# Storing g in five parts as it is made, and turning one chunk earlier

## The chip, the core and the metric

The kernel runs on one NeuronCore of a Trainium2 chip. The metric is the device time of one execution in microseconds. An execution of the profiled kind also leaves a trace: every instruction of every engine with its start and duration, every DMA packet, and the clock that TensorE was granted.

## What is computed

A retention block followed by a feed-forward block with squared ReLU. Cut to what matters:

```python
# q, k, v: (8, 8, 576, 64) float32 = batch, heads, sequence, head size
scores = q @ k.transpose(0, 1, 3, 2) / 8
Dmat = where(i >= j, gamma[h] ** (i - j), 0)          # causal decay, one gamma per head
x = ((scores * Dmat) @ v) -> (4608, 512)              # tokens x (heads * head size)
h = maximum(x @ w_in, 0)                              # w_in  (512, 2048)
out = (h * h) @ w_out                                 # w_out (2048, 512)
```

The two weight matrices arrive as 64-bit floats, so the kernel first makes 32-bit ones of them. The squared hidden layer is called g in the kernel.

## The kernel before, in words

**Retention.** Each of the 8 sequences is cut into four chunks of 128 tokens and one of 64, 40 chunks in all. A chunk's q and k are multiplied by powers of gamma (`scale_q`, `scale_v` on GpSimd; line 377 and 491), turned so that the head size lies across the partitions, multiplied with each other (`scores`), masked by VectorE (L484 or L543) and multiplied with v; a running state `u` carries what earlier chunks add. The first chunks are turned by TensorE (`turn_in`, L431) into PSUM and copied out by `turn_out` (L442: one half by ScalarE, one by VectorE); later ones are turned by VectorE (`flip`, L399) with small copies on ScalarE (L414). The result x goes, turned, to `xT` (L586).

**Weights.** The 64-bit weights come in pieces of 512 KB. A piece is converted in six steps (`round_parts`): two integer operations on VectorE (L212, L216), two operations on ScalarE (`beside`, L220 and L221), and three more on VectorE (L224, L227, L230). `convert(n)` emits the next n steps of the pieces of w_in in order. Pieces of w_out are converted later, summed, and kept in DRAM (`w2_dram`, stored at L283).

**First layer.** Tokens go in nine blocks of 512. Block 0 is multiplied directly (`first_in`, L714), piece by piece as w_in is converted. Blocks 1 to 8 use seven products in place of eight (`PRODUCTS`, `ffn_in`, L750): for each of four pairs of feature tiles `mp` there are seven steps `j`, each of eight matmuls of 128x128 by 256 columns. The steps' results are joined and squared into five parts of g: A11 (step 3: ScalarE L766, then squared by GpSimd L767), A22 (step 4: VectorE L769 and L757), S3 (step 5: L773, L757), A12 (step 6: L776, L757), and S1. Two sums follow, S1 = S3 + A22 (L690) and S3 = A11 - S3 (L691). The parts lie in `g_room`, which has room for two pairs, and go to `g_dram`.

**Second layer.** When all blocks are through, g is fetched again (`fetch_g`, L1016) and multiplied with w_out by the same seven products, once around and once within (`inner`, L1088). This part, from about 575 us on, touches neither edit.

**What sets the order.** The schedule is written out by hand: the order in which Python emits instructions is the order on each engine, and semaphores are added where one engine reads what another wrote. Chunks 0 to 3 and the first pieces of w_in are a plain list of calls (lines 889 to 947). From then on a loop over chunks takes a number of `step()`s of the first layer between the parts of a chunk's retention. Side work waits in `queue`; `some()` emits one entry of it in steps 6, 0, 1, 2 and 3. All loads and stores after the first three are issued by SyncE in the order of emission, so a store whose data are not ready holds up the loads behind it. In the trace SyncE has at most eight transfers under way: each issue waits for the landing of the eighth before it.

The loads for a chunk (`loads`) are emitted about three chunks before they are used.

## Time and profile before

| | us |
|---|---|
| time, median of three executions | 969.81 (969.76 to 970.41) |
| span of the profiled execution | 967.7 |
| TensorE busy | 949.6 |
| VectorE busy | 786.7 |
| ScalarE busy | 337.0 |
| GpSimd busy | 134.9 |
| bytes moved by DMA | 181.37 MB |
| g stores by `g_sums` | 32 of 1280 KB, 5.7 from issue to landing (median) |

Busy time is the time in which an engine had an instruction of the program under way. PE stands for TensorE's matmuls and PEld for its weight loads, DVE for VectorE, ACT for ScalarE, POOL for GpSimd, SP for SyncE; a q behind it (SPq) is its instruction queue. In the list of waits a line gives the engine and line that waited, what ended the wait, the total, the number of times and the longest. In a timeline a row gives start and duration in us, the engine, the line, the operation with output and input, the count, and in brackets the idle time before it with its releaser; "issue" means that the profile shows nothing the engine waited for. In a view by windows a row gives the stretch, its length, TensorE's busy time with the number of instructions, the granted clock as a share of the full one, the share of the DMA engines' time and the rate in GB/s.

### The profile page before, as it was taken

What the parts mean: (1) busy time and instruction counts of PE and PEld (TensorE: products, weight loads), DVE (VectorE), ACT (ScalarE), POOL (GpSimd) and SP (SyncE); (2) the same over time, 40 slices, a digit from 0 to 9 for tenths busy, and PEclk for the clock granted to TensorE, in tenths of its full rate; (3) what the DMA queues carried; (4) which work ended last, traced back from release to release, by engine and by line L of the source; (5) the groups of instructions that cost most, each with busy time, mean ns of one, the idle gap of its engine ahead of it and who ended that gap; (6) DMA issues with size and microseconds to landing.
All of it is one profiled execution on the core that took longest, in us unless ns stands there. A gap on an engine that the chain in (4) does not pass through costs nothing. (4 is left out here: it accounts for less than half of the span.)

```text
span 967.7 us, 23162 instructions
## 1 busy us (share of the span) xinstructions
PE 949.6 (98%) x9750; PEld 851.4 (88%) x9750; DVE 786.7 (81%) x1446; ACT 337.0 (35%) x807; POOL 134.9 (14%) x123
## 2 busy tenths in 40 slices
PE   8899999999999999989999999999999999999998
PEld 6654688888888888878888899999999999999998
DVE  5689799888799797977976597887888787887876
ACT  3354375856765766747721000000000000000000
POOL 3311323214223213222110000000000000000000
PEclk9999999999999999999999999999999999999999
DMA  9975567677757867755168966445354454525241
GB/s 230 239 215 138 151 180 197 192 238 197 199 153 223 242 162 190 230 168 169 61 247 333 358 244 266 149 159 185 122 196 160 159 198 166 199 100 174 88 175 44
DMA packets 170728, 181.37 MB, mean 187 GB/s; under 512 B 116864, under 2 KB 131200, under 8 KB 163968
## 3 DMA queue, kind: packets, MB, share of 16 engines
q1 hardware_dynamic: 168528, 179.37, 59.4%
q8 instruction: 76, 1.25, 0.5%
q10 hardware_dynamic: 2096, 0.52, 0.3%
q14 instruction: 28, 0.23, 0.1%
HBM read 109.36 MB, written 70.52 MB: 186 GB/s over the span
## 5 line engine op out<-in xcount | busy, mean ns | idle before, releaser
L750 PE MATMUL h_b<-room,w 128*128 128x256 f32 x768 | 184.7, 384 | 2.1 <-DVE room L769 1.8
L414 ACT COPY qk<-flip 32x256 f32<-32x256 f32 x416 | 167.4, 402 | 6.1
L750 PEld LDWEIGHTS h_b<-room,w 128*128 128x128 f32 x768 | 145.1, 191 | 24.5 <-DVE room L769 3.2
L1088 PE MATMUL o_b<-w,room 128*128 128x128 f32 x1168 | 144.4, 275 | 0.2 <-DVE room L1040 0.2
L1088 PEld LDWEIGHTS o_b<-w,room 128*128 128x128 f32 x1168 | 137.2, 192 | 0.4 <-DVE room L1040 0.4
L750 PE MATMUL h_a<-room,w 128*128 128x256 f32 x512 | 122.6, 382 | 2.7 <-issue 2.7
L1088 PE MATMUL o_c<-w,room 128*128 128x128 f32 x1008 | 123.0, 275 | 0.0
L750 PE MATMUL h_c<-room,w 128*128 128x256 f32 x512 | 121.7, 380 | 0.0
L1088 PEld LDWEIGHTS o_c<-w,room 128*128 128x128 f32 x1008 | 117.7, 192 | 0.0
L750 PEld LDWEIGHTS h_a<-room,w 128*128 128x128 f32 x512 | 96.6, 190 | 16.0 <-issue 2.6
L1102 ACT COPY r<-o_a 128x128 f32<-128x128 f32 x53 | 14.1, 265 | 271.7 <-PE o_a L1088 236.0
L750 PEld LDWEIGHTS h_c<-room,w 128*128 128x128 f32 x512 | 96.7, 190 | 13.3
L1088 PE MATMUL o_a<-w,a 128*128 128x128 f32 x688 | 85.6, 275 | 0.0
L767 POOL TENSOR_TENSOR room<-room 128x512 f32<-128x512 f32 x32 | 35.9, 1121 | 339.1 <-ACT room L766 339.1
L1088 PEld LDWEIGHTS o_a<-w,a 128*128 128x128 f32 x688 | 81.2, 192 | 0.1
L757 DVE SCALAR_TENSOR_TENSOR room<-room 128x512 f32<-128x512 f32 x96 | 70.7, 736 | 3.3
L714 PE MATMUL h_ps<-room,w 128*128 128x512 f32 (+2 forms) x160 | 60.7, 528 | 3.3 <-DVE w L230 3.0
L377 POOL TENSOR_TENSOR q_ld<-q_ld,dv 128x512 f32<-128x512 f32 (+1 forms) x39 | 46.2, 1185 | 85.2 <-DMA q_ld<-in_q_dram 77.5
L491 POOL TENSOR_TENSOR v_ld<-v_ld,dv 128x512 f32<-128x512 f32 (+1 forms) x40 | 53.5, 1338 | 6.7 <-DMA v_ld<-in_v_dram 6.7
L714 PEld LDWEIGHTS h_ps<-room,w 128*128 128x128 f32 x160 | 27.9, 199 | 27.5 <-issue 20.6
L609 PEld LDWEIGHTS x_ps<-qk,v_ld 64*64 64x64 f32 x1024 | 38.8, 134 | 13.0 <-issue 11.6
L769 DVE TENSOR_TENSOR room<-h_b,room 128x512 f32<-128x512 f32 x32 | 21.9, 685 | 33.5 <-PE h_b L750 33.5
(115 smaller groups left out, 1380.0 us busy)
## 6 DMA issues: line engine op xcount, KB each, us to landing
g_dram<-room SPq DMA_DIRECT2D x32, 1280.0 KB, 5.7
a<-g_dram SPq DMA_DIRECT2D x30, 1024.0 KB, 5.8
room<-g_dram SPq DMA_DIRECT2D x15, 1024.0 KB, 6.1
w<-w_dram SPq DMA_DIRECT2D x7, 1792.0 KB, 9.9
out_dram<-room SPq DMA_DIRECT2D x17, 512.0 KB, 3.3
q_ld<-in_q_dram SPq DMA_DIRECT2D x64, 128.0 KB, 5.3
w<-in_moe_w_in_dram SPq DMA_DIRECT2D x16, 512.0 KB, 6.3
w<-in_moe_w_out_dram SPq DMA_DIRECT2D x16, 512.0 KB, 4.2
```

The source lines that it names most:

```text
L377: engine.tensor_tensor(t, t, dv[:cs, :, NCH + ci:NCH + ci + 1].to_broadcast([cs, H, D]), op=ALU.mult)
L414: nc.scalar.copy(*moves.pop(0)[2:])
L491: nc.gpsimd.tensor_tensor(vs[:cs], vs[:cs], dv[:cs, :, ci:ci + 1].to_broadcast([cs, H, D]), op=ALU.mult)
L609: return [lambda hp=hp, e=e, b=b: nc.tensor.matmul(x_at(hp, e, b, h), lhsT=s["vs"][rows(h), head(hp, e), :], rhs=s["ret"][rows(h), e, hp, ...
L714: nc.tensor.matmul(p, lhsT=w[:, c, :], rhs=xT[0][:, c, :].rearrange("p (h t) -> p h t", h=2)[:, lo:hi, at[0]:at[1]], start=(c == 0), stop= ...
L750: nc.tensor.matmul(p[:, mm, :], lhsT=w[:, c, :], rhs=xs[n][right][:, c, :], start=(j in OPENS and mm == 0 and c == 0), stop=(j in CLOSES a ...
L757: nc.vector.scalar_tensor_tensor(t, t, 0.0, t, op0=ALU.max, op1=ALU.mult)
L767: nc.gpsimd.tensor_tensor(g["A11"], g["A11"], g["A11"], op=ALU.mult)
L769: nc.vector.tensor_tensor(g["A22"], p, p15, op=ALU.add)
L1088: nc.tensor.matmul(p, lhsT=s["lefts"][left][:, m, :], rhs=w_out[j][:, m, WO_SLOT[right], :], start=(i in OPENS and m == 0), stop=(i in CLO ...
L1102: nc.scalar.copy(r[:, 0, 0:128], p)
```

## The change

Two edits.

The first divides the store of g. Before, the last entry of `g_sums` stored all five parts of a pair at once, 1.28 MB. Now each part of 256 KB is stored in a step after it is made: A11 in step 5, A22 in step 6, A12 together with the sum S1, S1 together with the sum S3, and S3 last. The parts leave earlier and in smaller pieces, and the buffer's parts come free one by one.

The second moves chunk 3's turn in the list of calls. Before, four conversion steps of the third piece of w_in (`beside`, L224, L227, L230) stood ahead of it. Now the turn comes first, `beside` goes between turn and scores, and the three VectorE steps come after the scores. It is meant to let TensorE have the scores of chunk 3 without waiting for a conversion.

```diff
+    def g_store(n, mp, name):
+        nc.sync.dma_start(g_dram[n, G_KEPT.index(name), :, 2 * mp:2 * mp + 2, :], g_of(mp)[name])
+
     def g_sums(n, mp):
         g = g_of(mp)
         return [
-            lambda: nc.vector.tensor_tensor(g["S1"], g["S3"], g["A22"], op=ALU.add),
-            lambda: nc.vector.tensor_tensor(g["S3"], g["A11"], g["S3"], op=ALU.subtract),
-            lambda: nc.sync.dma_start(g_dram[n, :, :, 2 * mp:2 * mp + 2, :].rearrange("s p m t -> p s (m t)"),
-                                      g_room[mp % 2].rearrange("p s m t -> p s (m t)")),
+            lambda: [nc.vector.tensor_tensor(g["S1"], g["S3"], g["A22"], op=ALU.add), g_store(n, mp, "A12")],
+            lambda: [nc.vector.tensor_tensor(g["S3"], g["A11"], g["S3"], op=ALU.subtract), g_store(n, mp, "S1")],
+            lambda: g_store(n, mp, "S3"),
         ]
...
             queue.extend(g_sums(n, mp))
+
+        if j in (5, 6):
+            g_store(n, mp, "A11" if j == 5 else "A22")
...
     load(6)
-    convert(4)
     turn(3)
+    convert(1)
     scores_full(3)
     scale_q(4, nc.gpsimd)
+    convert(3)
     carry_full(3)
```

## The prediction

> **What bounds the kernel now.** I read the busy times first, then the list of TensorE's waits, then the timeline around the longest of them.

> The busy row of the page:
> ```profile
> PE 949.6 (98%) x9750; PEld 851.4 (88%) x9750; DVE 786.7 (81%) x1446; ACT 337.0 (35%) x807; POOL 134.9 (14%) x123
> ```
> TensorE works 949.6 of 967.7 us and no product is taken away. So the change can win only idle TensorE time, about 18 us, and time in which TensorE runs at a reduced clock, which counts as busy. TensorE's waits, total, times, longest:
> ```profile
> PE sc_ps L539 <- DVE qk L442: 3.6, 2, 3.4
> PE h_ps L714 <- DVE w L230: 3.0, 4, 1.2
> PE h_a L750 <- issue: 2.7, 1, 2.7
> PE h_b L750 <- DVE room L769: 1.8, 2, 1.3
> ```
> No line says that TensorE waited for a g store; the only reader of that kind is ScalarE, once, 1.3 us. Two single waits, 3.4 and 2.7 us, stand out.

> The first, in the timeline of TensorE (start, duration):
> ```profile
> 26.41 0.41 PE L431 MATMUL t_ps<-w,q_ld 64*128 64x64 f32 x8
> 30.18 1.16 PE L539 MATMUL sc_ps<-qk 64*128 64x128 f32 x16 [3.35 <-DVE qk L442]
> 31.27 1.13 PE L558 MATMUL x_ps<-qk,u_sb 64*64 64x128 f32 x16
> 32.33 3.14 PE L714 MATMUL h_ps<-room,w 128*128 128x128 f32 x16
> ```
> and of VectorE:
> ```profile
> 24.39 0.41 DVE L216 TENSOR_SCALAR w<-w 128x512 uint32<-128x512 uint32 x1
> 27.21 0.69 DVE L224 SCALAR_TENSOR_TENSOR w<-w,w 128x512 f32<-128x512 uint32 x1 [2.41 <-ACT w L220]
> 28.74 0.69 DVE L230 SCALAR_TENSOR_TENSOR w<-w,w 128x512 uint32<-128x512 uint32 x1
> 29.35 0.68 DVE L442 COPY qk<-t_ps 128x512 f32<-128x512 f32 x1
> ```
> Chunk 3 is transposed by 26.82, but VectorE copies it out only at 29.35: the copy stands behind three conversion steps, the first of which waits 2.41 us for ScalarE. After the gap the products are slow too: L558 takes 1.13 us here and 0.67 at 22.10; sixteen records of L714 take 3.14 here and 2.05 at 37.18. The windows show why (length, busy with its count, granted clock, DMA share, GB/s):
> ```profile
> 32.00:33.00 1.00, 1.00 (x11) 0.50 1.13 330
> 33.00:34.00 1.00, 1.00 (x7) 0.50 1.22 264
> ```
> and, after the second gap:
> ```profile
> 422.00:423.00 1.00, 1.00 (x4) 0.50 1.01 371
> ```
> The clock is halved in just two stretches before the end, each about 3.4 us long, one after each of the two gaps.

> The second gap has no releaser. TensorE's timeline, SyncE's, and the data queue between 410.94 and 416.6 us (packets, MB, share):
> ```profile
> 419.17 2.46 PE L750 MATMUL h_a<-room,w 128*128 128x256 f32 x8 [2.69 <-issue]
> ```
> ```profile
> 407.23 0.37 SPq L692 DMA_DIRECT2D g_dram<-room  x1
> 410.08 0.37 SPq L283 DMA_DIRECT2D w_dram<-w  x1
> ```
> ```profile
> q1 hardware_dynamic: 1128, 1.77, 101.9%
> ```
> Queue q8 carries instructions: 76 packets of 16 KB, and TensorE's 19,572 records make 76.5 blocks of 256. In the undisturbed last 350 us the k-th packet starts when TensorE is at record 256(k+0.64). Packet 37 should have started at 410.94; it started at 416.64, after 1.77 MB of data, took 1.03 us, and TensorE went on 1.5 us later. Until then it had run dry: it stopped at record 256(37+1.79), so packet k must be usable, 1.5 us after it ends, by 256(k+1.79). So this gap is a late instruction fetch, behind a g store of 1.28 MB (issued 407.23) and a store of converted weights of 1.34 MB (410.08).

> [...] A gap of 1.16 us at 19.85 to 21.01 us brought no drop. [...] here fetches waited until what was issued before them had gone (packet 18: a 1.79 MB store issued 0.25 us before its trigger, 7.17 us late; with nothing ahead, 0.8 to 1.3 us). [...]

> **Part 2: chunk 3's turn ahead of four conversion steps.** The order on VectorE becomes L216, copy L442, two mask products L543, then L224, L227, L230; ScalarE's copy likewise comes ahead of L220 and L221. Nothing is added. TensorE ends its transposes at 26.82; both copies start at once (at 7.92 and 7.95 they did so for chunk 0), VectorE's 0.69 us ends at 27.58, and the scores start 0.15 later, as now: 27.72 for 30.18, **2.46 us**. The gap left is 0.9 us, less than the 1.16 us that cost no clock, so L558 and L714 run at full speed: 1.13 - 0.67 and 3.14 - 2.05, **1.55 us**. Together 4.0.

> Who pays? The piece moved back (the third) ends at 32.2 to 33.0 us: masks from 28.88 to 30.17, then three steps of 0.6 to 1.5 us. Its reader, the third direct product, then stands at 39.80 - 4.0 = 35.8. The next piece would end some 5 us earlier than at present, against 4 for TensorE. Loads do not bind: the fifth and sixth chunks' q land at 36.39 and 40.12, and are turned at 43.7 and 53.5 even so.

> **Part 1: five stores.** Bytes and 2 KB rows are the same. Added: 128 issues at 0.37 us, 47 us of SyncE, which spends 151 us on issues between 110 and 575 us: nobody waits for it as such. A 256 KB store of g lands in 2.4 us (first quarters of block 0), the 1.28 MB one in 5.7. The buffers are rewritten two feature pairs later, over ten products of 1.73 us on, so the new waits of L690, L773 and L776 on landings, with the rest of VectorE's work queued behind them, are met long before; L769's such wait costs nothing visible now.

> SyncE's order does change. Three stores (A11, A22, A12) now stand ahead of a chunk's loads and wait for GpSimd and VectorE; behind them are q, k and v loads. At 410.5 the loads would move back to 416.7, when A12 is ready: 6 us. Who waits? GpSimd's scaling of q, which after 130 us begins 7 to 27 us after its landing, mostly over 10. At 117.65 the A11 store holds loads until 119.9, as GpSimd is itself waiting for q; k, landing at 125.8 now, is used at 130.26. So I charge nothing.

> The gain is at the late fetch. A22 and A12 leave by about 404 us, S1 and S3 by 404.5 and 407.2, so when the 1.34 MB store comes at 410.08 the queues are empty of g. That store remains whole ahead of the fetch: 1.34 MB at the 0.38 MB/us of its neighbouring slices is 3.5 us from 411.1, so the fetch begins near 414.7, is usable at 414.7 + 1.0 + 1.5 = 417.2, and TensorE, dry at 416.5, stands 0.7 us instead of 2.69: **2.0 us**. Such a short gap should not drop the clock: 2.46 - 1.99 and 3.05 - 1.89 for the two product groups after it, **1.7 us**. Bounds: nothing (the stall stays) and 2.7 + 1.7 = 4.4. Fetches with thin margins before that point (packets 17 and 31, 1.8 and 1.3 us) had g stores ahead of them, so they gain slack.

> Sum: 969.8 - 4.0 - 3.7 = **962.1 us**.

> **Rivals.** *Fetch still starved (0.20):* the weight store alone is enough to keep the gap and the clock drop; 969.8 - 4.0 = 965.8. For it: packet 18 was 7.17 us late with no g ahead. Against: the 0.4 MB of g ahead of packet 37 are gone. *Late loads (0.08):* moved back by 6 us, they reach VectorE's transposes late, as one k load does now (2.4 us at 116.5, without stopping TensorE); two or three such waits that do stop TensorE eat 1.5 to 4 us: 967.5 to 970. Against: the slack of 7 us or more. *Slower (0.06):* stores spread over the step lie ahead of more fetches; if the old stall stays and two more blocks starve at 4.4 us each, 965.8 + 8.8 = 974.6. Against: each store adds at most 0.7 us, and all fetches but three have over 2.7 us in hand.

> **How the numbers follow.** First forecast 0.66, around 962.1 (960.5 with the stall wholly gone plus some of VectorE's waits; 963.8 with half of it). It and the starved rival make 0.86, hence 960.5 to 966.3. Faster by over 0.2% means below 967.9: 0.66 + 0.20 and a third of the late loads, 0.89; same 0.05; slower 0.06.

> **What would show it.** The scores of chunk 3 start near 27.7 with a wait under 1 us, and the clock shows no drop near 31 to 35. The product that follows the gap at 419 comes 0 to 1 us after the one before, with no clock drop. Wrong would be: VectorE waiting for q or k loads, GpSimd's L767 late, or "issue" gaps on TensorE elsewhere.

## The result, and the profile after

| | before | after |
|---|---|---|
| time, median | 969.78 us (969.62 to 970.41, 4 runs) | 962.51 us (962.35 to 962.81, 4 runs) |
| ratio to before | | 0.9924 (0.9907 to 0.9941) |
| span of the profiled execution | 967.7 us | 960.6 us |

The change takes 7.3 us off; 7.7 were forecast, 962.1 us. The total came out closer than its parts: the term for the second gap was 1.1 us too large, and the profile of after is ahead by 0.7 us at its start, which no part of the change explains.

The busy row of the page of after, then TensorE's longest waits (total, times, longest):

```profile
PE 945.7 (98%) x9750; PEld 848.6 (88%) x9750; DVE 787.7 (82%) x1446; ACT 337.3 (35%) x807; POOL 135.4 (14%) x123
```
```profile
PE h_ps L716 <- DVE w L230: 2.2, 3, 1.6
PE h_a L752 <- issue: 1.8, 1, 1.8
PE h_b L752 <- DVE room L771: 1.8, 2, 1.3
PE sc_ps L539 <- DVE qk L442: 1.2, 2, 0.9
```

As many products as before, in 3.9 us less busy time: 3.2 us of that are the two stretches at half clock that are gone (the table below). Of the two waits that stood out, the one for chunk 3's scores has shrunk from 3.4 to 0.9 us; the one without a releaser is still there, at 1.8 us for 2.7.

Chunk 3 in TensorE's timeline, and in VectorE's (start, duration; idle time before in brackets):

```profile
25.69 0.41 PE L431 MATMUL t_ps<-w,q_ld 64*128 64x64 f32 x8
27.01 1.16 PE L539 MATMUL sc_ps<-qk 64*128 64x128 f32 x16 [0.91 <-DVE qk L442]
28.10 0.67 PE L558 MATMUL x_ps<-qk,u_sb 64*64 64x128 f32 x16
28.70 2.05 PE L716 MATMUL h_ps<-room,w 128*128 128x128 f32 x16
```
```profile
26.17 0.69 DVE L442 COPY qk<-t_ps 128x512 f32<-128x512 f32 x1 [1.53 <-PE t_ps L431]
...
29.38 0.68 DVE L224 SCALAR_TENSOR_TENSOR w<-w,w 128x512 f32<-128x512 uint32 x1
```

VectorE now waits for the transposes (1.53 us) instead of the reverse, copies at 26.17, and takes up the conversion, L224, after the masks. L558 and L716 take 0.67 and 2.05 us where they took 1.13 and 3.14. By windows (these rows have the busy times of all five engines; the clock is the third column from the right), the places of both old drops are at full clock:

```profile
33.00:34.00 1.00, 1.00 (x11) 1.00 (x10) 0.66 (x3) 1.00 (x3) 0.00 (x0) 1.00 1.35 229
415.00:416.00 1.00, 1.00 (x7) 0.87 (x6) 0.52 (x1) 0.31 (x1) 0.00 (x0) 1.00 0.77 174
```

The second gap in TensorE's timeline, SyncE's timeline ahead of it, and what the data queue moved between 406.39 us, when TensorE comes to record 256(37 + 0.64), at which the prediction's fit has fetch 37 due, and 411.36, when it starts:

```profile
413.77 1.46 PE L752 MATMUL h_a<-room,w 128*128 128x256 f32 x6 [1.84 <-issue]
```
```profile
403.18 1.17 SPq L687 DMA_DIRECT2D g_dram<-room  x2
405.54 0.37 SPq L283 DMA_DIRECT2D w_dram<-w  x1
406.44 6.07 SPq L687 DMA_DIRECT2D g_dram<-room  x3
```
```profile
q1 hardware_dynamic: 706, 1.93, 101.7%
```

The fetch still comes late, behind 1.93 MB in place of 1.77. It is 4.96 us late, not 5.69: the 1.77 MB included 624 packets of 256 bytes, pieces of loads, and went at 0.31 MB/us; the 1.93 had none and went at 0.39.

Where the time went, by comparing when TensorE reaches the same instruction in both traces:

| stretch | after is ahead by a further |
|---|---|
| up to 17 us, before either edit acts | 0.72 us |
| wait for chunk 3's scores | 2.45 us |
| first clock drop | 1.55 us |
| 60 to 95 us, TensorE waiting for conversions | -0.2 us |
| gap of fetch 37 | 0.85 us |
| second clock drop | 1.69 us |

The first row is no gain. The product of L714 (L716 in the changed kernel) that begins at 17.24 us before begins at 16.52 after; in six more profiles, of kernels that are the same up to there, it begins anywhere between 16.39 and 16.84 us. Between 60 and 95 us the lead rises and falls (5.54, 3.65, 4.50 us). A second profile of the changed kernel, `after_again` below, gains 0.1 us over the same stretch, so the -0.2 is no cost of the change either.

### The profile page after: what moved, and what is told of

Read it like the earlier page. It is cut to its first block, busy times and chain, and to the rows that moved or that the text cites. A ratio compares the mean times of both kernels' runs of the same rounds, so it can differ in the third digit from the quotient of the medians.

```text
span 960.6 us, 23424 instructions
## 1 busy us (share of the span) xinstructions
PE 945.7 (98%) x9750; PEld 848.6 (88%) x9750; DVE 787.7 (82%) x1446; ACT 337.3 (35%) x807; POOL 135.4 (14%) x123
## 5 line engine op out<-in xcount | busy, mean ns | idle before, releaser
L752 PE MATMUL h_b<-room,w 128*128 128x256 f32 x768 | 183.6, 382 | 2.1 <-DVE room L771 1.8
L752 PEld LDWEIGHTS h_b<-room,w 128*128 128x128 f32 x768 | 144.1, 190 | 23.9 <-DVE room L771 3.2
L752 PE MATMUL h_a<-room,w 128*128 128x256 f32 x512 | 122.0, 381 | 1.8 <-issue 1.8
L752 PE MATMUL h_c<-room,w 128*128 128x256 f32 x512 | 121.7, 380 | 0.0
L752 PEld LDWEIGHTS h_a<-room,w 128*128 128x128 f32 x512 | 96.4, 190 | 15.1 <-issue 1.7
L752 PEld LDWEIGHTS h_c<-room,w 128*128 128x128 f32 x512 | 96.7, 190 | 13.3
L769 POOL TENSOR_TENSOR room<-room 128x512 f32<-128x512 f32 x32 | 35.9, 1121 | 335.9 <-ACT room L768 299.4
L716 PE MATMUL h_ps<-room,w 128*128 128x512 f32 (+2 forms) x160 | 59.6, 518 | 3.5 <-DVE w L230 2.2
L716 PEld LDWEIGHTS h_ps<-room,w 128*128 128x128 f32 x160 | 26.8, 190 | 27.4 <-issue 20.7
```

Source lines behind the costliest of these rows:

```text
L716: nc.tensor.matmul(p, lhsT=w[:, c, :], rhs=xT[0][:, c, :].rearrange("p (h t) -> p h t", h=2)[:, lo:hi, at[0]:at[1]], start=(c == 0), stop= ...
L752: nc.tensor.matmul(p[:, mm, :], lhsT=w[:, c, :], rhs=xs[n][right][:, c, :], start=(j in OPENS and mm == 0 and c == 0), stop=(j in CLOSES a ...
L769: nc.gpsimd.tensor_tensor(g["A11"], g["A11"], g["A11"], op=ALU.mult)
```

## The experiments

Each kernel is set against runs of the kernel before on the same chip (medians 969.2 to 969.9 us).

**The two edits apart.** The first kernel has only the new place of the turn, the second only the five stores:

```diff
+    turn(3)
+    convert(1)
     scores_full(3)
     scale_q(4, nc.gpsimd)
+    convert(3)
```

> Chunk 3's turn moved, g still stored at once. Theory (the two edits act apart, the turn by 2.46 us of waiting and 1.55 us of halved clock): 969.8 - 4.0 = 965.8 us; the scores of chunk 3 wait about 0.9 us, the clock drop near 31 us is gone, and the gap of 2.7 us in the first layer (instruction fetch) with its clock drop is still there. Rival (VectorE is the bound between 48 and 110 us and gives the 4 us back there): 968.5 to 969.8. Rival (the gap in the first layer is a matter of chance and not of the stores): gap under 2 us without a clock drop, about 963.

> Five stores of g, chunk 3's turn where it was. Theory: the gap in the first layer shrinks from 2.7 to about 1.8 us and brings no clock drop, 0.9 + 1.7 = 2.6 us: 967.2 us; scores of chunk 3 still wait 3.3 us and the clock drops after it. Rival (the stores win by freeing buffers earlier or by easing the load on the queues all along): more than 2.6 us, with shorter waits in other places. Rival (the stores win nothing by themselves): 969.8.

The turn alone: 965.15 us (964.07 to 966.9), ratio 0.9957 (0.9944 to 0.997). The stores alone: 967.1 us (966.44 to 967.91), ratio 0.9973 (0.9963 to 0.9984). A line of the waits of the first kernel and a window of it, then the waits of the second:

```profile
PE h_a L750 <- issue: 2.7, 1, 2.7
```
```profile
417.00:418.00 1.00, 1.00 (x4) 0.81 (x3) 0.00 (x0) 0.75 (x2) 0.00 (x0) 0.50 1.04 381
```
```profile
PE sc_ps L539 <- DVE qk L442: 4.4, 2, 4.1
PE h_a L752 <- issue: 1.9, 1, 1.9
```

The parts separate: with the turn alone the gap of fetch 37 and its clock drop stay; with the stores alone the wait for the scores stays and the gap is 1.9. The gains, 4.2 and 2.3 us, sum to 6.5 of 7.3, which is within what these intervals tell. So the turn brought about 4 us, as forecast. The stores brought 2.3 us by time (1.6 to 3.6) and 2.5 by the table above, not 3.7.

**Is the gap a matter of where an instruction block ends?** Sixteen idle products of 32 columns, 64 instruction records of TensorE, move every later block boundary 64 records earlier. (A block is what one packet of q8 carries; over the last 350 us the packets start 255.7 records apart in the kernel before and 255.6 in the changed one.) A first pair put them into the warm-up in place of a product:

```diff
+    def small(count):
+        t = ps_f.tile([128, 512], F32, tag="f", name="idle_ps")
+        for _ in range(count):
+            nc.tensor.matmul(t[0:64, 0:32], lhsT=idle[:, 0:64], rhs=idle[:, 0:32], start=True, stop=True)
...
-    warm(5)
+    warm(4)
+    small(17)
```

> The kernel before with 64 more records on TensorE at its start, g stored at once and chunk 3 turned late as before. Theory (the gap of 2.7 us is a late instruction fetch and needs a block boundary at the end of a run of small products): gap and the clock drop after it go, 2.7 + 1.7 = 4.4 us: 965.4 us, the g stores being the same. Rival (the gap is the DMA backlog or the work itself): 969.8, gap at the same product.

> The changed kernel with 64 more records on TensorE at its start (one idle product of 256 columns gives way to 17 tiny ones), so that every boundary between instruction blocks lies 64 records earlier in the program. No DMA and no wait is changed. Theory (the remaining gap of 1.8 us is a late instruction fetch, at the boundary that falls at the end of a run of small products): the gap goes, 962.5 - 1.8 = 960.7 us; the shortest time between a fetch's trigger and its need is then 5.4 us, at places where fetches come 1 to 2 us late. Rival (the gap comes from the work itself): 962.5, gap in the same place.

Before with it: 966.45 us (964.91 to 968.79), ratio 0.9971 (0.996 to 0.9982). After with it: 961.85 us (960.47 to 963.4), ratio 0.9922 (0.9908 to 0.9935). In both the gap is gone, but the times are no clean measure. In the changed kernel with the small products in its warm-up the full clock came only at 13.4 us (6.0 without them), which put it 4.5 us behind by 13.7 us; in the kernel before, the early clock drop lasted two windows, 6.8 us, in the profiled run. So a second pair puts the same products where TensorE waits anyway:

```diff
+    small(8)
     first_in(0, (0,))
...
+    small(8)
     scores_full(2)
```

> The changed kernel with sixteen idle products of 32 columns put into two waits that TensorE has anyway (eight before the first product of piece 0, eight before the scores of chunk 2; 1.0 and 1.2 us of idle time there), so that every later instruction block of TensorE begins 64 instructions earlier, without the lost start of the run that shifted the blocks in the warm-up. If the 1.8 us gap that is left is set by where the block boundary falls among short products, it goes and nothing else changes: 962.5 - 1.8 = 960.7 us. If the extra products cost time on the path, they cost at most the 0.9 us each that they last: 962.5. If the gap does not depend on the place of the boundary, it stays: 962.5.

> The kernel before with the same sixteen idle products in the same two waits. If the block boundary makes the gap of 2.7 us and the gap makes the second clock drop, both go, and the first drop stays: 969.5 - 2.7 - 1.6 = 965.2 us. If the drop has another cause, 966.8. If the gap does not depend on the boundary, 969.5.

After with it: **960.77 us** (959.78 to 960.95), ratio 0.9911 (0.9897 to 0.9924). Before with it: 965.04 us (964.78 to 965.5), ratio 0.9957 (0.9945 to 0.997). The changed kernel beside them on the same chip:

> The changed kernel unchanged, beside the three others on one chip: 962.5 us, the gap of 1.8 us there, no clock drop.

962.71 us (961.82 to 963.89), ratio 0.9933 (0.9921 to 0.9946). TensorE's timeline of the shifted changed kernel:

```profile
15.47 1.07 PE L886 MATMUL idle_ps<-w 128*64 128x32 f32 x16
16.68 1.97 PE L716 MATMUL h_ps<-room,w 128*128 128x256 f32 x8
...
19.22 1.12 PE L886 MATMUL idle_ps<-w 128*64 128x32 f32 x16
20.45 1.16 PE L539 MATMUL sc_ps<-qk 64*128 64x128 f32 x16
```

The product of L716 comes at 16.68 and the scores at 20.45, against 16.52 and 20.29 in the changed kernel. The 0.16 us is less than the scatter at the start, and the 3.77 us between the two are the same: no cost of the idle products can be seen. Neither kernel has a TensorE wait with the releaser "issue" any more. Yet in the shifted changed kernel fetch 37 was 5.09 us late: not the lateness alone makes the gap but how soon the block is needed, and that depends on how many records of short products lie in the stretch. The changed kernel got from the record at which fetch 37 is due to the one at which it ran dry in 5.5 us; the same count of records took the shifted one 11.7 us. The pair also prices the whole gap: 969.22 to 965.04, 4.2 us in the kernel before, close to the sum of its gap and clock drop (2.7 + 1.7). In the changed kernel 1.9 us more were to be had, and this version beats both.

**What makes the gap drop the clock?** The kernel before, with three warm products of 512 columns in the 3.4 us wait for chunk 3's scores, and the warm-up shortened to keep the record count:

```diff
-    warm(5)
+    warm(2, 512)
...
     turn(3)
+    warm(3, 512)
     scores_full(3)
```

> The kernel before with three idle products of 512 columns (2.8 us) between chunk 3's turn and its scores; two idle products of 512 columns at the start stand for five of 256, so the number of records is the same. The scores still wait for VectorE's copy until about 30.2 us. Theory (the slow products after the gap are the clock[...]): no drop near 31 us, 1.55 us less: 968.2 us. Rival (they are slow for another reason, such as full DMA queues): 969.8, with L714 at 3.1 us again.

967.96 us (966.23 to 968.93), ratio 0.998 (0.9971 to 0.9989). TensorE's timeline:

```profile
31.52 0.67 PE L558 MATMUL x_ps<-qk,u_sb 64*64 64x128 f32 x16
32.11 2.05 PE L714 MATMUL h_ps<-room,w 128*128 128x128 f32 x16
```

The early drop is gone and the products after the scores run at full speed, with the scores no earlier (they begin at 30.42 us, and at 30.18 in the kernel before). So about 1.5 us of the first edit's gain are the clock's, and follow from the idle time. Its line for the second gap:

```profile
PE h_a L750 <- issue: 2.8, 1, 2.8
```

This time the 2.8 us gap cost no clock in 4 of 9 executions; in 5 it did. The median of all nine mixes the two kinds: the five with the second drop have a median of 968.26 us, 1.3 below the kernel before on that chip (969.56), and the four without lie at 966.2 to 967.2.

**Is it that the parts leave one by one, or that they leave early?** All five stores where the one store was:

```diff
-            lambda: g_store(n, mp, "S3"),
+            lambda: [g_store(n, mp, name) for name in G_KEPT],
```
(and none in the steps before).

> As the changed kernel, but the five stores of 256 KB are issued together in the last step, where the single store stood. Theory (what helps is that most of g has left before the weight store, not that the stores are small): gap of about 2.7 us with a clock drop, as with one store, so 965.8 us. Rival (small transfers let an instruction fetch in between): gap under 2 us without a drop, 962.5 to 963.2.

964.76 us (963.11 to 965.02), ratio 0.9945 (0.9932 to 0.9957). The gap was 2.0 us, between the 2.7 of one store and the 1.8 of five early ones, and the drop after it came in 2 of 5 executions. So neither expectation held as it stood. Cutting the store already helps, and the likely reason is that each part waits only for its own data: the first left 6.4 us before the fetch was due, the single store 3.7. The fetch was 5.18 us late, with all 1.38 MB of weights and 0.14 MB of load pieces ahead of it and hardly any g.

**Why is the gap 1.8 us and not 0.7?** My first theory: the loads that A12's store holds up until 399.6 push S1 and S3, and those push the weights. So A12's store was moved one entry later, behind the loads:

```diff
-            lambda: [nc.vector.tensor_tensor(g["S1"], g["S3"], g["A22"], op=ALU.add), g_store(n, mp, "A12")],
-            lambda: [nc.vector.tensor_tensor(g["S3"], g["A11"], g["S3"], op=ALU.subtract), g_store(n, mp, "S1")],
+            lambda: [nc.vector.tensor_tensor(g["S1"], g["S3"], g["A22"], op=ALU.add)],
+            lambda: [nc.vector.tensor_tensor(g["S3"], g["A11"], g["S3"], op=ALU.subtract), g_store(n, mp, "A12"), g_store(n, mp, "S1")],
```

> The changed kernel, with only the store of A12 moved one entry later, so that the loads of q, k and v stand ahead of it on SyncE's queue and leave before 399 us and not after it. Theory (the held-up loads push the stores of S1 and S3, those push the weight store of 405.5, and the instruction fetch starts when that store lands, 5.5 us after its issue): the weight store lands some 0.7 us sooner, the fetch starts at 410.7 and not 411.4, the gap of 1.8 us becomes 1.1; about 961.8 us. Rival (the weight store and the eight transfers under way set it alone, whatever their order): fetch delay 5.0 and gap 1.8 stay; 962.5.

962.45 us (961.95 to 962.68), ratio 0.9929 (0.9916 to 0.9941), no different from the changed kernel. SyncE's timeline:

```profile
394.88 2.66 SPq L150 DMA_DIRECT2D q_ld<-in_q_dram  x2
...
402.27 2.54 SPq L687 DMA_DIRECT2D g_dram<-room  x3
405.78 0.37 SPq L283 DMA_DIRECT2D w_dram<-w  x1
```

The loads did leave earlier, from 394.88, but the three stores stood behind them until 402.27; the fetch was 4.78 us late and the gap 1.6 us, for 4.80 and 1.5 in the changed kernel on that chip. The theory fell. Sorting the packets between the due time and the fetch by size then showed what was there: in the changed kernel 384 packets of 3584 bytes, the weights, 1.38 MB, and 268 of 2048 bytes, g, 0.55 MB. Of g only 0.09 MB passed in the first 2.2 us, the rest of the pair before; 0.46 passed in the second half, the A11 and A22 of the *next* pair, issued at 406.44 and 408.00. The last experiment keeps these two back, in this one pair alone, until A12 has left:

```diff
-            lambda: [nc.vector.tensor_tensor(g["S1"], g["S3"], g["A22"], op=ALU.add), g_store(n, mp, "A12")],
+            lambda: [nc.vector.tensor_tensor(g["S1"], g["S3"], g["A22"], op=ALU.add),
+                     [g_store(n, mp, name) for name in (("A12", "A11", "A22") if (n, mp) == (6, 0) else ("A12",))]],
...
-        if j in (5, 6):
+        if j in (5, 6) and (n, mp) != (6, 0):
```

> The changed kernel, in which for one pair alone (block 6, first pair) the stores of A11 and A22 wait until A12 has left, so that nothing of g leaves between 406.4 and 412 us. Between the moment in which instruction block 37 is due and its fetch the changed kernel moved 1.92 MB in 4.96 us: 1.38 of converted weights, 0.09 of the pair before and 0.46 of A11 and A22. Theory (the 0.46 MB shares the DMA engines with the weights and the fetch waits for both): 1.47 MB at 0.386 MB/us are 3.8 us, the fetch starts at 410.2, the gap is 0.6 us and not 1.8; about 961.4 us. Rival (the weight store lands 5.5 us after its issue whatever follows it, and the fetch waits for that landing alone): delay 4.7 to 5.0, gap 1.5 to 1.8; 962.5.

962.07 us (961.33 to 962.75), ratio 0.9922 (0.9909 to 0.9936). SyncE's timeline and the wait (this kernel is one line longer, so L753 is L752 of the changed one):

```profile
404.93 0.37 SPq L283 DMA_DIRECT2D w_dram<-w  x1
411.60 1.29 SPq L687 DMA_DIRECT2D g_dram<-room  x3
```
```profile
PE h_a L753 <- issue: 1.0, 1, 1.0
```

With nothing behind the weights, 1.49 MB moved, the fetch was 4.27 us late and the gap 1.0 us. Two profiles of the changed kernel have 4.96 and 4.80 us, and gaps of 1.8 and 1.5. So A11 and A22 account for 0.5 to 0.8 us of the gap. They did not slow the weights, as the theory had it: the weights' packets took 4.3 us here (405.83 to 410.11) and 4.2 in the changed kernel (406.43 to 410.61). But there the fetch began 0.75 us after the last of them (0.60 in the second profile), with packets of A11 and A22 in between, and here as they ended. The 0.3 to 0.4 us over the forecast of 0.6 stay. The time itself moved by no more than its spread, as a change this small must; this part rests on one profile of this kernel.

## Why the prediction was right, and where it was off

- **The turn: right in mechanism and size.** Wait 2.46 us forecast, 2.45 measured; clock 1.55 forecast, 1.55 measured; the edit alone gave 4.2 for 4.0. Filling the gap with other work returned the clock part alone. The piece moved back ended at 32.25 us (32.2 to 33.0 forecast), and the third direct product began at 35.08, 4.7 us sooner than before, so nobody paid for it in that stretch.
- **Five stores: right in mechanism, one term mis-sized.** The gap is a late instruction fetch behind data (5.69 us late before, 4.96 after): the shift of the block boundary removed it, 2.7 us in the kernel before and 1.8 in the changed one. The step that failed is the wait until the fetch, "3.5 us from 411.1, so the fetch begins near 414.7": that is 3.8 us after it is due, and it was 4.96. "The queues are empty of g" held for the pair before, of which only 0.09 MB was left. Two things were missed. First, the forecast looked only at what had been stored *before* the weights. Five stores leave earlier, so the next pair's A11 and A22 now come 0.9 and 2.5 us behind the weights, and 0.46 MB of them passed before the fetch, which began 0.75 us after the weights' last packet. Second, the weights took 4.2 us, not 3.5; a little of that is their size (1344 KB of 1024 bytes are 1.38 MB), and why they moved at 0.33 MB/us and not 0.38 stays open. The gap became 0.85 us shorter, not 2.0; of the 1.1 us between, 0.5 to 0.8 are the two stores by the last experiment.
- **The second clock drop: right.** 1.7 us forecast (the two differences named there sum to 1.63), 1.69 measured, although the gap left was 1.8 us and not the 0.7 on which the step rested. That was partly luck: 2.0 us gaps dropped the clock in 2 of 5 executions, and the last section shows how near 1.8 is to the edge.
- **Loads held up, charged at nothing: right.** VectorE's wait for a k load is 2.4 us once, in both kernels; of the "issue" gaps on TensorE there is just this one; and putting the loads first changed nothing. GpSimd shows four new waits on landings ahead of its squares (36.6 us in all), but its wait for ScalarE there fell from 339.1 to 299.4 us and TensorE shows no wait behind them.
- **Other fetches gain slack: right.** By the prediction's fit, the fetches with 1.8 and 1.3 us in hand had over 4 in after. The fit has TensorE run dry some ten records too late: in both traces the last record before the gap is number 9921, 256(37 + 1.75), not 256(37 + 1.79). Counted to there, the two had 0.8 and 0.3 us in hand before and over 3.5 after.
- **The rivals.** "Fetch still starved" was half right: the weights with what follows them do keep a gap, 1.8 us of it, but not the clock drop. Late loads and starved further blocks did not occur.

On the queues, the prediction went by its trace, in which fetches waited until what was issued before them had gone, and these runs side with it. In the last experiment, with 1.38 MB of weights as good as alone ahead of it, the fetch, due at 405.80, began at 410.07 us, as the last of their packets ended (410.11). In the changed kernel the fetch, due at 406.39 and begun at 411.36, also came behind 0.46 MB of two stores issued at 406.44 and 408.00, which is after it was due; why it waited for these as well was not shown.

## What to carry to other kernels

A TensorE gap that the profile puts down to "issue" may be an instruction block that waits behind data, as the 2.7 us before and the 1.8 after were here: count records to the block boundary, look at the transfers issued around the time it is due, both those before it and those that follow, and try moving the boundary by a few idle products inside an existing wait, which here took out the remaining 1.8 us of the gap at no cost that could be seen. Cutting a store so that it leaves earlier also moves the next one forward (here to 0.9 us behind the weights): ask what it will now run beside. When an engine that feeds TensorE has optional work in its queue, put what TensorE waits for ahead of it; the idle time and the clock drop behind it are two separate gains, here 2.45 and 1.55 us.

## What the runs showed of the hardware that I had not expected

Whether a gap halved the clock was a matter of chance over a range of lengths, here 2.0 to 2.8 us. One drop of 3.41 us makes a mean granted clock of 0.998, so the mean tells for every execution. Gaps of 1.0 to 1.9 us never did it: not in 19 executions of the changed kernel and of its two other store orders (0.999 or 1.000), nor the second gap of the stores alone in 8. At 2.0 us (five late stores) it happened in 2 of 5, at 2.7 (the turn alone) in 4 of 5, at 2.8 (the filled gap) in 5 of 9. Waits of 3.3 to 4.1 us did it in every profile that has one, in two of them for two windows (6.8 us). The kernel before shows 0.994 to 0.996 in all 46 executions run beside the experiments, two windows or more each; the mean does not tell which of its two gaps took them. The lengths are those of the profiled executions.

```profile
411.84:415.25 3.41, 0.84 (x4) 1.00 1.00 189
```
```profile
413.50:416.91 3.41, 1.93 (x127) 1.00 1.10 238
416.91:420.33 3.42, 2.09 (x10) 1.00 0.81 193
```

In the first the gap lies within one window, TensorE is idle for 75% of it, and the next window, 415.25 to 418.67, is at half clock (a part of it is shown with the first experiment). In the second the gap is split over two windows, idle for 43 and 39%, and nothing happens. With all thirteen traces cut in this way, TensorE was idle for 54 to 95% of the window ahead of every drop, and for at most 50% of any window at full clock that no drop followed. The one exception is a window of 57% in the last stretch of the kernel before. An estimate from these figures: a gap that stands alone should cost no drop below 1.7 us (half of the 3.413) and should cost one above 3.7 us (twice 54% of it), and between them it depends on where the window's edge falls. Of the 1.8 us in the changed kernel, 1.6 lay in one window, 46% of it.

The profile of a single execution therefore does not tell whether a gap of 2.0 to 2.8 us costs another 1.7 us, unless one looks at how it lies in the windows, and the next execution may lie differently.
